# Linear attention and two MLPs on one core: 128-byte operand starts, weights in two pools, single group last

## The chip, the cores and the metric

The kernel runs on one core of a Trainium2 chip. The metric is the device time of one execution in microseconds (us). It is measured over several runs; one more execution is recorded by the hardware profiler, and all rows below come from that one.

The engines are TensorE (PE; its weight loads are listed as PEld), VectorE (DVE), ScalarE (ACT), GpSimd (POOL) and SyncE (SP), which issues the DMAs. Each engine works through its own instruction queue in order.

## The reference

```python
q_s = exp(q - max(q, -1));  q_s = q_s / (sum(q_s, -1) + 1e-9)      # q, k, v: 8 x 8 heads x 576 x 64, float32
k_s = exp(k - max(k, 2));   k_s = k_s / (sum(k_s, 2) + 1e-9)
kv  = einsum('bhsd,bhse->bhde', k_s, v)
x   = einsum('bhsd,bhde->bhse', q_s, kv)       # -> 4608 tokens x 512
h   = x @ w_in;  r = maximum(h, 0);  x = (r * r) @ w_out           # 512 -> 2048 -> 512, weights float64
g   = x @ w_gate;  val = x @ w_val                                 # 512 -> 1536
out = (g / (1 + exp(-g)) * val) @ w_out2                           # 1536 -> 512
```

## The kernel before

**First MLP.** The 4608 tokens go through in 9 blocks (`NB`) of 512 (`T`), the hidden width in 16 slices (`NF`). Every operand is kept as a high and a low part, and one product is three matmuls (`mm3`, L109). For each slice `f` of a block, `h_mm` makes 12 matmuls of 128x512 into the bank `ph`; `g_of` takes relu and square on ACT and splits the result into `g`, the low part on DVE (L104); one slice later `acc_mm` makes 12 matmuls into the four banks `acc`. The attention of the next block is worked in between by a plan.

**Weights.** The class `Weights` loads a raw float64 tile, takes its bits apart on ACT and DVE (`bits`, L136 to L146) and splits it on ACT and POOL (`split`, L187 and L189), all of this in block 0. The 32 split tiles live in the pool `wp` (32 slots of 4 KB per partition). The first 18 raw loads, and k, v and q of block 0, borrow slots of `wp` that no weight has taken yet; later raw loads go through `raws`, which has two buffers. Blocks 1 to 7 prepare the second MLP's weights (`operands`) and write them to DRAM.

**From one MLP to the other.** `x2_store` (L454) copies the four `acc` banks of a block to SBUF, two on ACT (L462) and two on DVE (L460), and SP stores each to DRAM `x2d` (L463). At the last block, 8, the attention's pools on the right side of SBUF are closed and `x1`, `wr` and `xs` take their place; from then on SP may fetch. The pools of the left side (`wr2`, `x2`, `st`, `uo`, `u`) lie where `wp` and its neighbours were, and open only when the first MLP is done.

**Second MLP.** It runs over groups of blocks with a scheme of seven products (order 1, 5, 6, 2, 7, 3, 4). The first group is the single block 0, and four pairs of blocks follow. `XOperands` loads a group's parts of `x2d` (L534) and makes its operands `xo` on ACT and DVE (L104, and `xt` and `x` in L542 to L552): in the last block of the first MLP for the first group, in the output stage of the group before for every other. `gated` makes 504 matmuls, 512 wide for a pair and 256 wide for the single; the two operands of a matmul are a slot `wu` and an `xo`. `out_stage` makes 504 (a pair) or 252 (the single), 256 wide, from `wu` and `uo`; each `uo` is split on ACT and DVE just before. `Stream` fetches `wu` tiles of 512 KB, 63 a group: 42 for `gated`, each used by 12 matmuls, and 21 for `out_stage`, each used by 24 (a pair) or 12 (the single). It runs up to 9 ahead (`LEAD`): of any nine consecutive tiles the first three (`EARLY`) lie in `wr`, the other six in `wr2`. Between the two MLPs `prime` writes one matmul into each of the eight banks (L571).

**What sets the order.** SP works in the order of the source. On the other engines a scheduler orders the instructions by readiness and program order when the kernel is built.

**Where tiles lie.** In the built program the pools of the left side start at multiples of 128 bytes in a partition. `pad` is the first allocation of the right side and shifts all that follow: with 8 floats it takes 64 bytes, so that `raws`, `cv` (bits), `stp`, `kp`, `qp`, `qtp`, and later `x1`, `wr` and `xs` start 64 bytes past a multiple of 128.

Of the kernel before, what the change touches and what calls it, by code (L numbers as in the profile page):

```python
# [17 lines left out]
P = 128  # L18
# [4 lines left out]
def tile_linear_attention_two_mlps(  # L23
# [34 lines left out]
    T = 512  # L58
# [15 lines left out]
    ph1 = ExitStack()  # L74
    wp = ph1.enter_context(tc.tile_pool(name="wp", bufs=2 * NF))
    rp = ph1.enter_context(tc.tile_pool(name="rp", bufs=2))
# [6 lines left out]
    pad = ctx.enter_context(tc.tile_pool(name="pad", bufs=1, side="right"))  # L83
    pad.tile([P, 8], F32, name="pad")
    raws = ph0.enter_context(tc.tile_pool(name="raws", bufs=2, side="right"))
# [65 lines left out]
    class Weights:  # L151
# [8 lines left out]
        def load(self):  # L160
            if self.n_load == len(self.order):
                return
            key = self.order[self.n_load]
            self.n_load += 1
            kind, f = key
            w = self.src[kind]
            if self.n_load <= self.borrow:
                t = w_slot(wp).rearrange("p t n -> p (t n)").bitcast(w.dtype)
            else:
                t = raws.tile([P, T], w.dtype, name="wraw", tag="wraw")  # L170
            raw_load(w, kind == "out", f, t)
            self.raw[key] = t
# [7 lines left out]
        def split(self, n):  # L180
            todo = []
            for key in self.order[self.n_split:min(self.n_split + n, self.n_bits)]:
                t = self.done[key] = w_slot(wp)
                self.n_split += 1
                todo.append((t, self.mid.pop(key)))
            for t, w in todo:
                nc.scalar.copy(t[:, 0], w)  # L187
            for t, w in todo:
                nc.gpsimd.tensor_tensor(t[:, 1], w, f32(t[:, 0]), op=ALU.subtract)  # L189
# [11 lines left out]
    def w_slot(pool):  # L201
        return pool.tile([P, 2, T], F32R, name="w", tag="w")
# [4 lines left out]
        + [x for f in range(NF) for x in (("out", f), ("in", f + 2)) if x[1] < NF],  # L207
        18,
    )
# [244 lines left out]
    def x2_store(i, d):  # L454
# [6 lines left out]
        else:  # L461
            nc.scalar.copy(e, acc.pop((i, d)))  # L462
        nc.sync.dma_start(x2d[i][:, d], e)  # L463


    groups = [(0,)] + [(i, i + 1) for i in range(1, NB, 2)]
    pools = {}
# [99 lines left out]
    def prime():  # L567
        t = stream.slots[0]
        banks = [bank() for _ in range(8)]
        for ps in banks:  # L570
            nc.tensor.matmul(  # L571
                ps, lhsT=t[:, 0, 0, 0:P], rhs=t.rearrange("p u t n -> p (u t n)")[:, 0:T],
                start=True, stop=True,
            )

# [109 lines left out]
    with tc.manual_schedule(engines={mybir.EngineType.SP}):  # L685
# [5 lines left out]
        def borrowed():  # L691
            return f32(w_slot(wp)).rearrange("p t n -> p (t n)")

# [20 lines left out]
        for hp, (n_kv, n_q, n_t, n_x) in enumerate(steps):  # L714
            plan.append((n_kv, lambda hp=hp: kv_unit(0, hp)))
            plan.append((n_q, lambda hp=hp: q_unit(0, hp)))
            plan.append((n_t, lambda hp=hp: q_transpose(0, hp, w_slot(wp))))
            plan.append((n_x, lambda hp=hp: x_pair(0, hp)))
# [9 lines left out]
        for n in range(NB * NF + LAG):  # L728
            i, f = divmod(n, NF)
            a = divmod(n - LAG, NF) if n >= LAG else None  # L730
            if i < NB:
                if f == 0:
# [6 lines left out]
                    if i == NB - 1:  # L739
# [3 lines left out]
                        for name, bufs in (("x1", 14), ("wr", EARLY), ("xs", 5)):  # L743
                            pools[name] = ctx.enter_context(
                                tc.tile_pool(name=name, bufs=bufs, side="right", reuse_waits="tile")
                            )
                        xo = XOperands(0)
                        xo.load(0)
                        for _ in range(EARLY):
                            stream.fetch()  # L750
                        steps = xo.all_steps()
                ph = h_mm(i, f)
# [4 lines left out]
                elif i < NB - 1 and n >= NF + 2:  # L757
                    next(work, None)
                if i == NB - 1 and f >= 2:
                    next(steps, None)  # L760
            if a and not (f == 0 and i < NB):
# [19 lines left out]

        prime()
        for _ in steps:
            pass
# [45 lines left out]
```

## Time and profile before

| | us |
|---|---|
| median of 3 runs (1749.21 to 1750.91) | 1750.1 |
| the profiled execution | 1751.04 |
| its span, first to last instruction | 1749.3 |
| PE busy in it | 1700.5 |
| DVE / ACT / POOL busy | 960.0 / 803.8 / 304.3 |

The profiled execution's time is 1.74 us longer than its span, and 0.9 us above the median. By the timeline, block 0 of the first MLP fills the first 160 us, the blocks 1 to 8 reach to 933 us, the single group to 1035 us, and each pair takes some 177 us after that. The mean granted clock of TensorE is 0.994 of full speed; a clock of 1.00 in a window is its higher level, 2.4 GHz, and 0.50 its lower one, 1.2 GHz.

### The profile page before, as it was taken

To read this page: it belongs to the slowest core of one execution; us is meant where nothing else is said; L and a number is where in the kernel's file an instruction comes from. 1 tells how busy PE (TensorE), PEld (TensorE's weight loads), DVE (VectorE), ACT (ScalarE), POOL (GpSimd) and SP (SyncE) were. 2 spreads that over 40 slices of the span, in tenths; PEclk is the share of its full clock that TensorE was granted. 3 is DMA by queue.
4 is the path that set the end of the run, shared out by engine and by line. 5 is a ranking of instruction groups with operands and counts; after the bars stand their busy time and mean duration, and the time that the engine had idled before them with its cause. 6 is when DMAs were issued, how large, how long until landed. Compare 5 with 4: busy or idle time off the path is not lost.

```text
span 1749.3 us, 25146 instructions
## 1 busy us (share of the span) xinstructions
PE 1700.5 (97%) x9420; PEld 1436.6 (82%) x9420; DVE 960.0 (55%) x1626; ACT 803.8 (46%) x1435; POOL 304.3 (17%) x279
## 2 busy tenths in 40 slices
PE   5889999999999999999999999999999999999999
PEld 4667888888888888888788988899889988998889
DVE  8997465555555555543412654475446544654455
ACT  5655444555555454554433453354335433543343
POOL 3552211112120211211001201210111011101110
PEclk9999999999999999999999989999999999999999
DMA  9344433434443343332206996668666866686663
GB/s 260 99 122 124 118 113 108 142 113 144 127 124 118 110 161 109 120 103 93 82 0 241 404 318 192 194 208 251 191 192 207 256 190 190 212 255 191 187 191 121
DMA packets 192969, 292.12 MB, mean 167 GB/s; under 512 B 87248, under 2 KB 124112, under 8 KB 192848
## 3 DMA queue, kind: packets, MB, share of 16 engines
q1 hardware_dynamic: 192848, 290.51, 53.3%
q8 instruction: 75, 1.23, 0.3%
q14 instruction: 46, 0.38, 0.1%
HBM read 238.55 MB, written 51.90 MB: 166 GB/s over the span
## 4 chain that ended last, share of the span: by engine, by line
PE 87%; DVE 4%; DMA 2%; issue 1%; ACT 1%; POOL 1%; SPq 0%; DVEq 0%; POOLq 0%; ACTq 0%
PE ps L109 45%; PE ph L109 20%; PE acc L109 20%; PE pa L339 1%; PE pa L374 1%; DVE wbits L142 1%; DVE wbits L146 1%; DMA wraw<-in_moe_w_out_dram 0%; POOL w L189 0%; DVE wbits L138 0%; DVE g L104 0%; DMA wu<-gvd 0%; DVE xo L104 0%; DMA x2d<-r 0%; DMA kt<-in_k_dram 0%
## 5 line engine op out<-in xcount | busy, mean ns | idle before, releaser
L109 PE MATMUL ps<-xo,wu 128*128 128x512 f32 (+1 forms) x2520 | 529.5, 372 | 0.1
L109 PEld LDWEIGHTS ps<-xo,wu 128*128 128x128 f32 x2520 | 439.2, 188 | 89.4 <-DMA wu<-gvd 0.3
L109 PE MATMUL acc<-g,w 128*128 128x512 f32 x1728 | 437.2, 398 | 5.5 <-DVE g L104 3.9
L109 PE MATMUL ph<-xT,w 128*128 128x512 f32 x1728 | 421.9, 393 | 10.1 <-POOL w L189 5.5
L109 PEld LDWEIGHTS ph<-xT,w 128*128 128x128 f32 x1728 | 321.1, 188 | 83.7 <-POOL w L189 7.6
L109 PEld LDWEIGHTS acc<-g,w 128*128 128x128 f32 x1728 | 318.4, 189 | 78.7 <-DVE g L104 8.3
L109 PE MATMUL ps<-wu,uo 128*128 128x256 f32 x2268 | 275.8, 284 | 4.4 <-DVE uo L104 3.1
L109 PEld LDWEIGHTS ps<-wu,uo 128*128 128x128 f32 x2268 | 274.3, 192 | 6.0 <-DVE uo L104 4.1
L104 DVE TENSOR_TENSOR g<-r,g 128x512 fp32r<-128x512 f32 x144 | 110.8, 770 | 187.9 <-ACT g L103 187.4
L442 ACT ACTIVATE r<-ph 128x512 f32<-128x512 f32 x144 | 85.8, 596 | 242.4 <-PE ph L109 235.0
L103 ACT CAST uo<-u 128x512 fp32r<-128x512 f32 (+1 forms) x210 | 119.2, 577 | 130.2 <-PE ps L109 88.2
L633 DVE TENSOR_TENSOR u<-u,ps 128x512 f32<-128x512 f32 (+1 forms) x60 | 38.0, 634 | 253.3 <-ACT u L632 253.0
L104 DVE TENSOR_TENSOR uo<-u,uo 128x512 fp32r<-128x512 f32 (+1 forms) x210 | 135.7, 657 | 63.8 <-ACT uo L103 63.4
L638 POOL TENSOR_TENSOR u<-u 128x512 f32<-128x512 f32 (+1 forms) x30 | 35.5, 1183 | 766.2 <-DVE u L634 627.9
L588 ACT COPY ps<-ps 128x512 f32<-128x512 f32 x126 | 71.9, 570 | 112.9 <-PE ps L109 110.9
L443 ACT ACTIVATE r<-r 128x512 f32<-128x512 f32 x144 | 91.1, 633 | 3.4
L103 ACT CAST g<-r 128x512 fp32r<-128x512 f32 x144 | 89.0, 618 | 3.3
L233 POOL TENSOR_TENSOR wsum<-wbits 128x256 f32<-128x256 f32 x36 | 35.0, 984 | 254.0 <-DVE wbits L146 198.9
L359 POOL TENSOR_TENSOR qs<-qs,qm 128x512 f32<-128x512 f32 x32 | 37.5, 1173 | 210.0 <-DVE qm L358 186.7
L189 POOL TENSOR_TENSOR w<-wbits,w 128x512 fp32r<-128x512 f32 x32 | 51.1, 1601 | 54.8 <-ACT w L187 49.1
L632 ACT ACTIVATE u<-ps 128x512 f32<-128x512 f32 (+1 forms) x60 | 33.3, 555 | 56.6 <-PE ps L109 56.5
L605 DVE TENSOR_TENSOR s<-ps,p 128x512 f32<-128x512 f32 x63 | 43.2, 690 | 26.8 <-PE ps L109 23.4
(99 smaller groups left out, 1383.2 us busy)
## 6 DMA issues: line engine op xcount, KB each, us to landing
wu<-gvd SPq DMA_DIRECT2D x210, 512.0 KB, 4.4
wu<-od SPq DMA_DIRECT2D x105, 512.0 KB, 4.0
gvd<-wst SPq DMA_DIRECT2D x84, 256.0 KB, 2.3
od<-wst SPq DMA_DIRECT2D x42, 256.0 KB, 2.3
wraw<-in_moe_w_out_dram SPq DMA_DIRECT2D x20, 512.0 KB, 4.3
x<-x2d SPq DMA_DIRECT2D x32, 256.0 KB, 6.0
kt<-in_k_dram SPq DMA_DIRECT2D x28, 288.0 KB, 3.3
vt<-in_v_dram SPq DMA_DIRECT2D x56, 144.0 KB, 3.7
```

The costliest lines, as they stand in the source:

```text
L103: nc.scalar.copy(hi, src)
L104: (eng or nc.vector).tensor_tensor(lo, src, f32(hi), op=ALU.subtract)
L109: nc.tensor.matmul(ps, lhsT=w[s], rhs=x[t], start=start and n == 0, stop=stop and n == 2, skip_group_check=more,)
L189: nc.gpsimd.tensor_tensor(t[:, 1], w, f32(t[:, 0]), op=ALU.subtract)
L233: nc.gpsimd.tensor_tensor(to, x, y, op=op)
L359: nc.gpsimd.tensor_tensor(t, t, m.unsqueeze(3).to_broadcast([P, TJ, 2, D]), op=ALU.subtract)
L442: nc.scalar.activation(r, ph, AF.Relu)
L443: nc.scalar.activation(r, r, AF.Square)
L588: nc.scalar.copy(x, y)
L605: nc.vector.tensor_tensor(x, y, z, op=ALU.add)
L633: nc.vector.tensor_tensor(u, u, gate, op=ALU.mult)
L638: nc.gpsimd.tensor_tensor(s1, a21, a22, op=ALU.add)
```

## The change

1. The pad takes 24 floats (128 bytes) instead of 8. All pools of the right side move by 64 bytes: `x1`, `wr`, `xs`, `raws`, `cv`, `stp`, `kp`, `qp` and `qtp` now start at multiples of 128. The attention's `kv` and `vt`, which stood there, are now 64 past.
2. The pool `wp` becomes two of 16 slots. `wpa` holds the weights of slices f < 8 and the borrowed raw loads (16 instead of 18), `wpb` those of f >= 8 and block 0's borrowed k, v, q and transposed q. `wr2`, `x2` and `st` lie on `wpa`, `uo` and `u` on `wpb` and above, so that the slots of `wr2` and `x2` come free halfway through block 8.
3. The groups are four pairs, and then block 8 alone. The first group is thus a pair: its operands are 512 wide, the loads 256 KB, and it needs the 14 tiles of `x2`.
4. The operands of the first group are emitted after the first MLP, not between the slices of block 8.
5. `x2_store` of block 8 issues its DMAs from ACT, not from SP.
6. `prime` writes two matmuls into the banks `pa` at the start of block 8, not eight into the second MLP's banks.

```diff
--- before.py
+++ after.py
@@ -72,7 +72,8 @@
     const = ctx.enter_context(tc.tile_pool(name="const", bufs=1))
     dram = ctx.enter_context(tc.tile_pool(name="dram", bufs=1, space=DRAM))
     ph1 = ExitStack()
-    wp = ph1.enter_context(tc.tile_pool(name="wp", bufs=2 * NF))
+    wpa = ph1.enter_context(tc.tile_pool(name="wpa", bufs=NF))
+    wpb = ph1.enter_context(tc.tile_pool(name="wpb", bufs=NF))
     rp = ph1.enter_context(tc.tile_pool(name="rp", bufs=2))
     gp = ph1.enter_context(tc.tile_pool(name="gp", bufs=2))
     xp = ph1.enter_context(tc.tile_pool(name="xp", bufs=NP))
@@ -81,7 +82,7 @@
     ps_a = ph1.enter_context(tc.tile_pool(name="ps_a", bufs=2, space=PSUM))
     ph0 = ExitStack()
     pad = ctx.enter_context(tc.tile_pool(name="pad", bufs=1, side="right"))
-    pad.tile([P, 8], F32, name="pad")
+    pad.tile([P, 24], F32, name="pad")
     raws = ph0.enter_context(tc.tile_pool(name="raws", bufs=2, side="right"))
     cv = ph0.enter_context(tc.tile_pool(name="cv", bufs=5, side="right"))
     stp = ph0.enter_context(tc.tile_pool(name="stp", bufs=1, side="right"))
@@ -165,7 +166,7 @@
             kind, f = key
             w = self.src[kind]
             if self.n_load <= self.borrow:
-                t = w_slot(wp).rearrange("p t n -> p (t n)").bitcast(w.dtype)
+                t = w_slot(wpa).rearrange("p t n -> p (t n)").bitcast(w.dtype)
             else:
                 t = raws.tile([P, T], w.dtype, name="wraw", tag="wraw")
             raw_load(w, kind == "out", f, t)
@@ -180,7 +181,7 @@
         def split(self, n):
             todo = []
             for key in self.order[self.n_split:min(self.n_split + n, self.n_bits)]:
-                t = self.done[key] = w_slot(wp)
+                t = self.done[key] = w_slot(wpa if key[1] < NF // 2 else wpb)
                 self.n_split += 1
                 todo.append((t, self.mid.pop(key)))
             for t, w in todo:
@@ -205,7 +206,7 @@
         {"in": w_in, "out": w_out},
         [("in", 0), ("in", 1)]
         + [x for f in range(NF) for x in (("out", f), ("in", f + 2)) if x[1] < NF],
-        18,
+        NF,
     )
 
 
@@ -460,10 +461,10 @@
             nc.vector.tensor_copy(e, acc.pop((i, d)))
         else:
             nc.scalar.copy(e, acc.pop((i, d)))
-        nc.sync.dma_start(x2d[i][:, d], e)
-
-
-    groups = [(0,)] + [(i, i + 1) for i in range(1, NB, 2)]
+        (nc.scalar if i == NB - 1 else nc.sync).dma_start(x2d[i][:, d], e)
+
+
+    groups = [(i, i + 1) for i in range(0, NB - 1, 2)] + [(NB - 1,)]
     pools = {}
     EARLY = 3
     LEAD = 9
@@ -565,13 +566,10 @@
 
 
     def prime():
-        t = stream.slots[0]
-        banks = [bank() for _ in range(8)]
-        for ps in banks:
-            nc.tensor.matmul(
-                ps, lhsT=t[:, 0, 0, 0:P], rhs=t.rearrange("p u t n -> p (u t n)")[:, 0:T],
-                start=True, stop=True,
-            )
+        w, x = w1.pair(("in", 0), 0), xT[NB - 1, 0]
+        for _ in range(2):
+            ps = ps_a.tile([P, T], F32, name="pa", tag="pa")
+            nc.tensor.matmul(ps, lhsT=w[0], rhs=x[:, 0], start=True, stop=True)
 
     def quarters(product, n):
 
@@ -689,7 +687,7 @@
 
 
         def borrowed():
-            return f32(w_slot(wp)).rearrange("p t n -> p (t n)")
+            return f32(w_slot(wpb)).rearrange("p t n -> p (t n)")
 
         for hp in range(NP):
             kt = borrowed()[:CK, 0:2 * NC * D].rearrange("p (h c d) -> p h c d", h=2, c=NC)
@@ -714,7 +712,7 @@
         for hp, (n_kv, n_q, n_t, n_x) in enumerate(steps):
             plan.append((n_kv, lambda hp=hp: kv_unit(0, hp)))
             plan.append((n_q, lambda hp=hp: q_unit(0, hp)))
-            plan.append((n_t, lambda hp=hp: q_transpose(0, hp, w_slot(wp))))
+            plan.append((n_t, lambda hp=hp: q_transpose(0, hp, w_slot(wpb))))
             plan.append((n_x, lambda hp=hp: x_pair(0, hp)))
         plan += [(5, lambda: w1.step(1)), (8, lambda: w1.step(1))]
         tick = run_at(plan)
@@ -744,11 +742,11 @@
                             pools[name] = ctx.enter_context(
                                 tc.tile_pool(name=name, bufs=bufs, side="right", reuse_waits="tile")
                             )
+                        prime()
                         xo = XOperands(0)
                         xo.load(0)
                         for _ in range(EARLY):
                             stream.fetch()
-                        steps = xo.all_steps()
                 ph = h_mm(i, f)
                 tick(2 * f)
                 g_of(i, f, ph)
@@ -756,8 +754,6 @@
                     w1.step(1)
                 elif i < NB - 1 and n >= NF + 2:
                     next(work, None)
-                if i == NB - 1 and f >= 2:
-                    next(steps, None)
             if a and not (f == 0 and i < NB):
                 for d in range(NP):
                     acc_mm(*a, d)
@@ -779,8 +775,7 @@
             tc.tile_pool(name="ps", bufs=8, space=PSUM, reuse_waits="tile")
         )
 
-        prime()
-        for _ in steps:
+        for _ in xo.all_steps():
             pass
         for g in range(len(groups)):
             ops, steps, after = [], iter(()), None
```

The order of the instructions moves with it at three places. The first is PE (a) and ACT (b) between the MLPs and after; `acc` and `ph` are banks of the first MLP, `ps` those of the second, and `xN` counts like instructions in a row. PE before, from the last slice of block 8 to the second pair:

```order
L109 MATMUL ph<-xT,w 128x512 x12
L109 MATMUL acc<-g,w 128x512 x24
L571 MATMUL ps<-wu 128x512 x8
L109 MATMUL ps<-xo,wu 128x256 x504
L109 MATMUL ps<-wu,uo 128x256 x252
L109 MATMUL ps<-xo,wu 128x512 x504
L109 MATMUL ps<-wu,uo 128x256 x504
L109 MATMUL ps<-xo,wu 128x512 x504
```

PE now, over the rest of the program:

```order
L110 MATMUL ph<-xT,w 128x512 x12
L110 MATMUL acc<-g,w 128x512 x24
L110 MATMUL ps<-xo,wu 128x512 x504
L110 MATMUL ps<-wu,uo 128x256 x504
L110 MATMUL ps<-xo,wu 128x512 x504
L110 MATMUL ps<-wu,uo 128x256 x504
L110 MATMUL ps<-xo,wu 128x512 x504
L110 MATMUL ps<-wu,uo 128x256 x504
L110 MATMUL ps<-xo,wu 128x512 x504
L110 MATMUL ps<-wu,uo 128x256 x504
L110 MATMUL ps<-xo,wu 128x256 x504
L110 MATMUL ps<-wu,uo 128x256 x252
```

The eight matmuls of `prime` are gone from between the MLPs, and the single group's 256-wide gated matmuls stand last. ACT at the same place before (the copies of `acc` for `x2d`, and then the seeding of banks):

```order
L442 ACTIVATE r<-ph 128x512
L443 ACTIVATE r<-r 128x512
L103 CAST g<-r 128x512
L462 COPY r<-acc 128x512 x2
L588 COPY ps<-ps 128x512
L597 COPY p_8220<-ps 128x512
L588 COPY ps<-ps 128x512
```

ACT now:

```order
L444 ACTIVATE r<-r 128x512
L104 CAST g<-r 128x512
L463 COPY r<-acc 128x512
L464 DMA x2d_125<-r 128x512 x2
L463 COPY r<-acc 128x512
L464 DMA x2d_125<-r 128x512 x2
L586 COPY ps<-ps 128x512 x2
L595 COPY p_8230<-ps 128x512
L595 COPY p_8231<-ps 128x512
```

The stores of block 8 (`x2d_125`) stand in ACT's queue between the copies and the first seeding. SP at the start of block 8, before (`x2d_114` is block 0, `x2d_121` and `x2d_122` are blocks 7 and 8):

```order
L534 DMA x<-x2d_114 128x256 x4
L487 DMA wu<-gvd_123 128x1024 x3
L463 DMA x2d_121<-r 128x512 x4
L534 DMA x<-x2d_114 128x256 x4
L463 DMA x2d_122<-r 128x512 x4
L487 DMA wu<-gvd_123 128x1024 x4
L487 DMA wu<-gvd_124 128x1024 x7
```

SP now (`x2d_117`, `x2d_118` and `x2d_124` are blocks 0, 1 and 7):

```order
L535 DMA x<-x2d_117 128x512
L535 DMA x<-x2d_118 128x512 x2
L535 DMA x<-x2d_117 128x512
L488 DMA wu<-gvd_126 128x1024 x3
L464 DMA x2d_124<-r 128x512 x4
L535 DMA x<-x2d_117 128x512
L535 DMA x<-x2d_118 128x512 x2
L535 DMA x<-x2d_117 128x512
L488 DMA wu<-gvd_126 128x1024 x4
L488 DMA wu<-gvd_127 128x1024 x7
```

Eight loads of 128 KB have become eight of 256 KB, and no store stands between the loads and the fetches of `wu`. DVE in the second half of block 8, before, where the operands of the single group (128x256) go on past the copies for block 7's store:

```order
L104 TENSOR_TENSOR g<-r,g 128x512
L545 TENSOR_TENSOR x<-x 128x256
L104 TENSOR_TENSOR xo<-x,xo 128x256
L104 TENSOR_TENSOR g<-r,g 128x512
L104 TENSOR_TENSOR xo<-xt,xo 128x256
L547 TENSOR_TENSOR x<-x 128x256
L104 TENSOR_TENSOR xo<-x,xo 128x256
L552 TENSOR_TENSOR x<-x 128x256
L104 TENSOR_TENSOR xo<-x,xo 128x256 x4
L104 TENSOR_TENSOR g<-r,g 128x512 x13
L460 COPY r<-acc 128x512 x2
```

DVE now, in the slices f 8 to 15 of block 8:

```order
L105 TENSOR_TENSOR g<-r,g 128x512
L105 TENSOR_TENSOR xo<-x,xo 128x512
L543 TENSOR_TENSOR xt<-x 128x512
L546 TENSOR_TENSOR x<-x 128x512
L105 TENSOR_TENSOR xo<-xt,xo 128x512
L548 TENSOR_TENSOR x<-x 128x512
L105 TENSOR_TENSOR xo<-x,xo 128x512
L553 TENSOR_TENSOR x<-x 128x512
L105 TENSOR_TENSOR xo<-x,xo 128x512
L105 TENSOR_TENSOR g<-r,g 128x512
L105 TENSOR_TENSOR xo<-x,xo 128x512 x3
L105 TENSOR_TENSOR g<-r,g 128x512 x5
```

The first `g` here is that of slice 9. Nine operand steps stand just before it, behind the `g` of slice 8; eight stand between it and the next, and three behind that one.

## Rows read from the trace of the kernel before

**Rows 1.** page, part 1 busy time, and part 4 the chain by line.

```profile
PE 1700.5 (97%) x9420; PEld 1436.6 (82%) x9420; DVE 960.0 (55%) x1626; ACT 803.8 (46%) x1435; POOL 304.3 (17%) x279
...
PE ps L109 45%; PE ph L109 20%; PE acc L109 20%; PE pa L339 1%; PE pa L374 1%; DVE wbits L142 1%; DVE wbits L146 1%; DMA wraw<-in_moe_w_out_dram 0%; POOL w L189 0%; DVE wbits L138 0%; DVE g L104 0%; DMA wu<-gvd 0%; DVE xo L104 0%; DMA x2d<-r 0%; DMA kt<-in_k_dram 0%
```

**Rows 2.** windows, PE alone: us, PE busy (matmuls touched), granted clock, DMA share, GB/s.

```profile
870.00:930.00 60.00, 60.00 (x266) 1.00 0.00 1
1050.00:1150.00 100.00, 100.00 (x433) 1.00 0.66 200
1160.00:1200.00 40.00, 40.00 (x338) 1.00 0.70 223
```

**Rows 3.** windows, PE, cut at weight slots: gated pair (two), output stage (two).

```profile
1070.24:1086.78 16.54, 16.54 (x72) 1.00 0.63 186
1087.01:1095.04 8.03, 8.03 (x36) 1.00 0.66 186
1153.76:1162.29 8.53, 8.53 (x72) 1.00 0.57 184
1162.40:1170.77 8.37, 8.37 (x73) 1.00 0.57 180
```

**Rows 4.** timeline, first MLP to second: start us, us, what, [idle before <-releaser].

```profile
...
933.29 0.85 PE L571 MATMUL ps<-wu 128*128 128x512 f32 x3
...
935.75 1.42 PE L571 MATMUL ps<-wu 128*128 128x512 f32 x5 [1.61 <-DVE r L460]
...
937.01 5.22 PE L109 MATMUL ps<-xo,wu 128*128 128x256 f32 x39
...
941.61 0.54 PEld L109 LDWEIGHTS ps<-xo,wu 128*128 128x128 f32 x4 [0.33 <-DMA wu<-gvd]
```

**Rows 5.** timeline of PE, output stage of the single group.

```profile
996.75 5.50 PE L109 MATMUL ps<-wu,uo 128*128 128x256 f32 x44
...
1005.08 24.84 PE L109 MATMUL ps<-wu,uo 128*128 128x256 f32 x190 [0.20 <-DVE uo L104]
...
1033.12 2.50 PE L109 MATMUL ps<-wu,uo 128*128 128x256 f32 x10 [2.37 <-DVE uo L104]
1035.42 4.88 PE L109 MATMUL ps<-xo,wu 128*128 128x512 f32 x13
```

**Rows 6.** chain of waits inside that output stage: start us, us, what.

```profile
...
999.19 1.14 DVE xt L542
...
1029.12 1.21 DVE xo L104 x2
...
```

**Rows 7.** windows, PE alone: transition, single group, first pair, a later pair.

```profile
933.00:942.00 9.00, 7.26 (x49) 1.00 0.78 241
950.00:990.00 40.00, 40.00 (x342) 1.00 1.03 408
1010.00:1020.00 10.00, 10.00 (x86) 1.00 0.94 301
1035.10:1038.50 3.40, 3.40 (x11) 0.50 0.95 304
1213.00:1223.00 10.00, 10.00 (x51) 1.00 0.80 249
```

**Rows 8.** start of the last block: timeline of PE, and the page's DMA issues.

```profile
856.12 2.11 PE L109 MATMUL ph<-xT,w 128*128 128x512 f32 x8 [1.27 <-ACT r L442]
...
x<-x2d SPq DMA_DIRECT2D x32, 256.0 KB, 6.0
...
x<-x2d SPq DMA_DIRECT2D x8, 128.0 KB, 3.2
```

**Rows 9.** timeline of DVE, late in the last block.

```profile
924.48 0.69 DVE L104 TENSOR_TENSOR g<-r,g 128x512 fp32r<-128x512 f32 x1 [4.75 <-ACT g L103]
```

**Rows 10.** timeline of ACT at the end.

```profile
1744.71 1.30 ACT L678 COPY o<-ps 128x512 f32<-128x512 f32 x2 [7.30 <-PE ps L109]
```

**Rows 11.** windows, all engines, block 0: PE, PEld, DVE, ACT, POOL busy, clock, DMA.

```profile
0.00:160.00 160.00, 124.91 (x653) 93.00 (x653) 140.26 (x224) 89.53 (x161) 72.08 (x61) 0.97 0.57 154
```

## The prediction

> **What bounds the kernel now.** I read the page first: PE is busy 1700.5 of 1749.3 us, and 85% of the chain that ended last are three lines of matmuls [rows 1]. So a term counts only if it shortens matmuls, or fills a gap between them; DVE, ACT and the DMA queue matter where PE waits for them. The other views serve to find both. Windows of PE alone give the spacing of matmuls in each stage: the first MLP makes 266 of 512 columns in 60 us, a pair's gated stage 433 in 100 us, its output stage 338 of 256 columns in 40 us [rows 2]. A window also counts the matmuls that it cuts, one too many, so these are 60/265 = 226.4 ns, 100/432 = 231.5 ns and 40/337 = 118.7 ns. Timelines then show where PE stands still: between the MLPs [rows 4], in the single group's output stage [rows 5], and at the start of block 8 [rows 8]. I sum against the profiled execution's 1751.04 us, and take 0.9 off at the end, since the median lies so much lower.
>
> **Alignment (change 1).** In the first MLP all operands of a matmul start at multiples of 128 bytes. In a gated stage `xo` of `x1` lies 64 bytes past, and the slot alternates: the 72 matmuls on six `wr2` slots, which are aligned, took 16.54 us, the 36 on three `wr` slots, 64 past like `x1`, took 8.03 us [rows 3]. These windows run from the first start to the last, so there are 71 and 35 spacings: 232.9 and 229.4 ns. In the output stage `uo` is aligned: with `wr2`, all aligned, 8.53/71 = 120.1 ns; with `wr`, mixed, 8.37/71 = 117.9 ns (72 starts, and one cut) [rows 3]. So for 512 columns a mixed pair is the slowest, for 256 it is the fastest. After the change everything in the second MLP is aligned.
> The pairs' 2016 gated matmuls go from 231.6 ns (2/3 of 232.9 and 1/3 of 229.4 make 231.7; the long window said 231.5) to a value that this trace shows in the first MLP alone: 226.4 would give 2016 x 5.2 = 10.5 us, the 229.4 of two operands displaced alike 4.4 us, and no effect 0. I take 227.5, nearer to the one row in which all is aligned, since that row has the same shape and three-product pattern: 2016 x 4.1 = **-8.3 us**.
> The 256-wide ones lose. A third of the 2268 output matmuls are on `wr`: 756 x 2.2 = 1.7 us. The single's 504 gated ones took from 937.01 to 996.75, 59.74 us [rows 4, 5], less 0.3 of waiting 117.9 ns each; at 120.1 they cost 1.1 us more. Sum **+2.8 us**; bounds 0 to 2.8. Net **-5.5 us**, between -10.5 and +2.8.
> Other engines and DMAs on these pools I cost at nothing: only PE is on the path, and its spacing in the gated stage is the same at a DMA share of 0.63 and 0.66 [rows 3].
> The Trainium skill, page "SBUF — State Buffer", section "Specifications (TRN2)", says that a partition is read in lines of 16 bytes, and that bandwidth is lost where a line isn't hit at least twice. By that a start at 64 is as good as one at 128, and this term would be 0. The trace speaks against it: rows of one shape and engine differ by 1.5 and 1.9% with the slot alone [rows 3].
>
> **Between the MLPs (changes 2, 5, 6).** Before, the last `acc` matmul ends where `prime` begins, at 933.29; three go, PE waits 1.61 us for the DVE copy of the last bank, which waited for a store, five more go, and the first real one starts at 937.01; at 941.61 a weight load waits 0.33 us for a `wu`, whose fetch stood behind the stores in SP's queue [rows 4]. That is 3.7 + 0.3 = 4.0 us. After, the first product needs the banks of the first two copies, which are out by 933, and `wu` tiles that have long been there. What is next late: the seeding copies on ACT, now behind the block's last copy and store in ACT's own queue (its order stands ahead). Product 1 is 12 matmuls, 2.75 us, and lasts to 936.05; the next in line waits for the seeds. ACT copies the last bank at about 934.3 as before (it waits for the same buffer), and then the issue and two copies of 0.57 us follow, done by 936.75: a wait of 0.7 us (0 if the scheduler's next product goes first, 1.5 if the issue on ACT takes longer). The two matmuls of `prime` at the start of block 8 cost 0.46 us if nothing hides them. Net -4.0 + 0.7 + 0.5 = **-2.9 us** (-4.0 to -1.5).
>
> **The single group last (change 3).** Its output stage makes 252 matmuls of 256 columns. They ran from 996.75 to 1035.42, 38.67 us [rows 5], where 252 x 118.7 ns = 29.9 us would do: 8.7 us lost. The next group's first matmuls ran at a granted clock of 0.50 from 1035.10 to 1038.50 [rows 7]: 3.4 us for 1.7 us of work. Sum 10.4 us. The chain inside that stage is DVE at `xt`, `x` and `xo` of the following pair [rows 6], 512 wide, which stand ahead of the single's own `uo`: the next group's operands are a pair's, and the cover is half a pair's long. From pair to pair the same work is covered: 1213 to 1223 shows PE full at clock 1.00 [rows 7]. After, the single is followed by nothing, and the pair before it has to make only half-width operands. I take all of it, **-10.3 us** (-10.4 to -8).
>
> **Start of block 8 (changes 3, 4).** SP loads 4 x 256 KB before the `wu` fetches and block 7's stores, instead of 4 x 128 KB; such a load took 6.0 us instead of 3.2 [rows 8]. The stores land later by up to the difference of the transfer, half of 2.8 us, since the loads overlap: +1.4. The copies of block 7's last banks wait for them, then `g`, then PE, which waited 1.27 us there [rows 8]. The next loads and the steps of c = 1 no longer stand ahead of `g` there, -0.6. Together **+0.8 us** (0 to +2).
>
> **Middle of block 8 (change 4).** Nine operand steps stand on DVE between the `g` of slices 8 and 9, eight more before slice 10. A `g` takes 0.69 us, and DVE then waits 4.75 us for the next [rows 9]; nine steps of 0.69 take 6.2 us, 1.5 more than the gap. Since a slice's `acc` matmuls come one slice later, PE has 12 matmuls, 2.7 us, before it needs that `g`. So covered, but for the loads of c = 1, which six `wu` fetches press on: **+0.3 us** (0 to +2.5).
>
> **The end.** PE stops, two banks are copied on ACT one after the other (1.30 us [rows 10]) and stored. With the single there is one: **-0.3 us**. **Block 0** is paced by DVE, 140.26 of 160 us, with PE at 124.91 [rows 11]; weights now wait for other slots, two raw loads more go through `raws`, and q loads of the next block stand behind them on SP. The first split may come earlier. I find nothing that makes a sign: **0 us**, between -3 and +3.
>
> **Sum.** -5.5 - 2.9 - 10.3 + 0.8 + 0.3 - 0.3 = -17.9: 1751.04 - 17.9 = 1733.1, on the median's footing **1732 us**.
>
> **Rivals.**
> (a) The alignment brings nothing, neither gain nor loss: 5.5 more, 1738. Against it, the slots' rows; for it, that the two operands displaced alike [rows 3] are not the slowest.
> (b) The gated stage reaches the first MLP's spacing fully: 2.2 less, and with the seeds in time 1729.
> (c) The single's stalls belong to its half-length products, and move to the end with it; change 3 doesn't do what it seems to: 10.3 more, 1742. Against it, the names in the chain [rows 6], none of them its own but `uo`.
> (d) Slower: the single group at the end starves. Its 63 tiles are 33.0 MB for 504 x 120 + 252 x 119 ns = 90 us; nine are there ahead, so 54, 28.3 MB, must come at 314 GB/s. In 950 to 990 it got 408 GB/s with PE full, at a DMA share of 1.03, which is all there is; in 1010 to 1020 301 GB/s [rows 7]. At 301 it takes 94 us, 4 us more. It decides from 262 GB/s: 28.3 MB then take 108 us, all 17.9 us are gone, and any less is slower than before, 1752 at 257. Nothing in the rows is so low while PE waits for `wu`.
> (e) The clock falls between the MLPs, where no `prime` keeps PE at work: some 3.4 us at half speed as in 1035.10 to 1038.50 [rows 7], 1.7 more, 1734. For it, the 2.37 us without work ahead of that stretch [rows 5]. Against it, the wait of 1.61 us between the MLPs, after which the clock stayed at 1.00 [rows 4, 7]; the wait that I expect is shorter. [...]
>
> **How the numbers follow.** Forecast 0.62, (a) 0.12, (b) 0.09, (c) 0.08, (d) 0.03, (e) 0.06. The low end takes the alignment at its bound and a gain in block 0: 1732 - 5 - 2 = 1725; the high end takes (a) with block 0 against it: 1738 + 3 = 1741. Outside lie (c), (d) and some tails, 0.2 in all. A difference under 0.2%, 3.5 us, could not be told from no change. All but (d) lie below 1746.6; with tails: faster 0.93, same 0.04, slower 0.03.
>
> **What would show it.** Right: gated windows of pairs at about 440 matmuls in 100 us, PE without a gap between product 1 and the last `acc`, the output stages full from the first pair to the end, no clock below 1.00 behind 160 us. Wrong: gated windows still at 433; gaps in the single's output stage with no `xo` in their chain; weight loads that wait for `wu` in the last 90 us; a first MLP's block 0 that ends later than at 160 us.

## The result, and the profile after

The changed kernel takes 1732.4 us in the median of 4 runs (1730.23 to 1733.91), the kernel before 1749.65 beside it: a ratio of 0.9901, 95% interval 0.9884 to 0.9918. The forecast was 1732. The profiled execution of the changed kernel has a span of 1732.1 us at a mean granted clock of 0.998. It lies 17.2 us below the span before, and the accounts below are made between these two spans. The profiled execution was the slowest of the four runs, at 1733.9 us; on that footing the forecast was 1733.1.

From the page of the changed kernel, the busy time of each engine and the chain by line; they answer to [rows 1]:

```profile
PE 1686.0 (97%) x9414; PEld 1434.3 (83%) x9414; DVE 960.6 (55%) x1626; ACT 803.7 (46%) x1435; POOL 297.8 (17%) x279
...
PE ps L110 45%; PE ph L110 21%; PE acc L110 19%; PE pa L340 1%; DVE wbits L147 1%; DVE wbits L143 1%; PE pa L375 1%; POOL w L190 1%; DMA x2d<-r 1%; DVE wbits L139 1%; DVE m L320 1%; DVE g L105 0%; DMA wraw<-in_moe_w_out_dram 0%; ACT wbits L137 0%; DMA x<-x2d 0%
```

PE is still what the kernel consists of: 14.5 us less of PE's time, and 2.7 us less without it.

Windows of PE alone (us, PE busy and matmuls touched, granted clock, DMA share, GB/s): the stretch between the MLPs, a pair's gated stage, a pair's output stage, and the single's two stages, which now end the program. They answer to [rows 2] and [rows 7]:

```profile
933.00:945.00 12.00, 11.24 (x49) 1.00 0.39 132
1120.00:1220.00 100.00, 100.00 (x443) 1.00 0.69 205
1060.00:1100.00 40.00, 40.00 (x336) 1.00 0.73 226
1640.00:1690.00 50.00, 50.00 (x419) 1.00 0.98 366
1698.00:1727.00 29.00, 29.00 (x244) 1.00 0.81 299
```

443 matmuls in 100 us where 433 were, so 226.2 ns each, or 226.7 by a stage's own length (114.27/504; before 116.85/504 = 231.8); in the output stage 60.48/504 = 120.0 ns, before 60.17/504 = 119.4. The single group runs at 366 GB/s with PE full, and its output stage, 244 in 29 us, has no gap.

The program by stages. Each boundary is the first matmul of a stage in a timeline of PE, in block 1 the first `g` on DVE:

| stage | before, us | after, us | difference |
|---|---|---|---|
| start to first `g` of block 1 | 166.43 | 169.48 | +3.05 |
| from there to the second MLP's first matmul | 770.58 | 767.94 | -2.64 |
| four gated stages of pairs | 469.13 | 458.13 | -11.00 |
| four output stages of pairs | 240.85 | 241.89 | +1.04 |
| gated stage of the single | 59.74 | 60.48 | +0.74 |
| output stage of the single | 38.67 | 30.40 | -8.27 |
| end of PE to end of span | 3.90 | 3.78 | -0.12 |
| sum | 1749.3 | 1732.1 | -17.2 |

Timeline between the MLPs after (start, length, what, and in brackets the idle time before with its releaser), the place of [rows 4]:

```profile
...
937.42 2.88 PE L110 MATMUL ps<-xo,wu 128*128 128x512 f32 x12
938.67 0.59 ACT L463 COPY r<-acc 128x512 f32<-128x512 f32 x1 [2.54 <-DMA x2d<-r]
939.29 1.11 ACTq L464 DMA_DIRECT2D x2d<-r  x2
939.35 0.69 DVE L461 COPY r<-acc 128x512 f32<-128x512 f32 x1 [2.42 <-DMA x2d<-r]
...
940.44 1.06 ACT L586 COPY ps<-ps 128x512 f32<-128x512 f32 x2 [1.18 <-PE ps L110]
...
941.07 2.11 PE L110 MATMUL ps<-xo,wu 128*128 128x512 f32 x8 [0.76 <-ACT ps L586]
```

There is no `prime` and no gap ahead of the first product. ACT's queue is as forecast: copy, two stores, where the second waits for DVE's copy at 939.35, and only then the seeding copies; PE waits 0.76 us for these at 941.07.

Block 8 after, its start, the place of [rows 8]:

```profile
...
857.76 1.79 PE L110 MATMUL acc<-g,w 128*128 128x512 f32 x6 [1.31 <-ACT r L463]
860.54 2.09 PE L110 MATMUL ph<-xT,w 128*128 128x512 f32 x8 [0.99 <-ACT r L443]
...
```

and its middle, PE and then DVE; the gap ahead of `g` in [rows 9] is filled:

```profile
...
910.24 2.76 PE L110 MATMUL acc<-g,w 128*128 128x512 f32 x11 [0.21 <-DVE g L105]
...
```

```profile
...
903.48 0.69 DVE L543 TENSOR_TENSOR xt<-x 128x512 f32<-128x512 f32 x1 [0.38 <-DMA x<-x2d]
904.81 0.69 DVE L546 TENSOR_TENSOR x<-x 128x512 f32<-128x512 f32 x1 [0.63 <-DMA x<-x2d]
...
909.50 0.68 DVE L105 TENSOR_TENSOR g<-r,g 128x512 fp32r<-128x512 f32 x1
...
```

DVE waits 0.38 and 0.63 us for `x` loads of c = 1, `g` of slice 10 comes at 909.50, and PE waits 0.21 us for it.

Block 0, DVE's first `g` of block 1 and SP's last raw load of the first MLP's weights; the first stood at 166.43 before, the other at 143.31:

```profile
169.48 0.69 DVE L105 TENSOR_TENSOR g<-r,g 128x512 fp32r<-128x512 f32 x1 [3.49 <-ACT g L104]
```

```profile
...
146.62 0.35 SPq L118 DMA_DIRECT2D wraw<-in_moe_w_out_dram  x1
```

### The profile page after: what moved, and what is told of

Same layout as the page of the kernel before. It is cut to its first block, busy times and chain, and to the rows that moved or that the text cites. A ratio compares the mean times of both kernels' runs of the same rounds, so it can differ in the third digit from the quotient of the medians.

```text
span 1732.1 us, 25141 instructions
## 1 busy us (share of the span) xinstructions
PE 1686.0 (97%) x9414; PEld 1434.3 (83%) x9414; DVE 960.6 (55%) x1626; ACT 803.7 (46%) x1435; POOL 297.8 (17%) x279
## 4 chain that ended last, share of the span: by engine, by line
PE 88%; DVE 5%; DMA 2%; ACT 2%; issue 2%; POOL 1%; SPq 0%; ACTq 0%; POOLq 0%; DVEq 0%
PE ps L110 45%; PE ph L110 21%; PE acc L110 19%; PE pa L340 1%; DVE wbits L147 1%; DVE wbits L143 1%; PE pa L375 1%; POOL w L190 1%; DMA x2d<-r 1%; DVE wbits L139 1%; DVE m L320 1%; DVE g L105 0%; DMA wraw<-in_moe_w_out_dram 0%; ACT wbits L137 0%; DMA x<-x2d 0%
## 5 line engine op out<-in xcount | busy, mean ns | idle before, releaser
L110 PE MATMUL ps<-xo,wu 128*128 128x512 f32 (+1 forms) x2520 | 518.7, 368 | 0.8 <-ACT ps L586 0.8
L110 PE MATMUL ph<-xT,w 128*128 128x512 f32 x1728 | 427.4, 396 | 13.6 <-POOL w L190 5.6
L105 DVE TENSOR_TENSOR g<-r,g 128x512 fp32r<-128x512 f32 x144 | 106.7, 741 | 183.1 <-ACT g L104 182.8
L190 POOL TENSOR_TENSOR w<-wbits,w 128x512 fp32r<-128x512 f32 x32 | 45.9, 1438 | 68.8 <-ACT w L188 66.3
L595 ACT COPY p<-ps 128x512 f32<-128x512 f32 x63 | 37.0, 588 | 42.6 <-PE ps L110 41.7
```

The costliest lines, as they stand in the source:

```text
L105: (eng or nc.vector).tensor_tensor(lo, src, f32(hi), op=ALU.subtract)
L110: nc.tensor.matmul(ps, lhsT=w[s], rhs=x[t], start=start and n == 0, stop=stop and n == 2, skip_group_check=more,)
L595: nc.scalar.copy(x, y)
```

## The experiments

Each kernel ran beside the kernel before on the same chip. Times are medians, and in brackets stands the median of the kernel before on that chip, which is 1748.3 to 1749.65 us. Differences to the changed kernel are taken from its 1732.4; counted by the distance to the kernel before beside each, they come out up to 1.4 us larger.

**Alignment alone, on the kernel before.**

```diff
-    pad.tile([P, 8], F32, name="pad")
+    pad.tile([P, 24], F32, name="pad")
```

> The kernel before with one edit: the pad takes 24 floats. Theory (alignment sets the spacing of matmuls): the 2016 gated 512-wide matmuls of the pairs go from 231.8 to 226.7 ns each, -10.3 us; the 256-wide ones lose 2 us; 1749.6 becomes about 1741.5, and block 1's first g stays at 166 us. Rival 1 (the spacing came from the new order or the pools): gated spacing stays at 231.8, time 1749.6. Rival 2 (the 3 us that block 0 lost came with the moved raw and bits tiles): spacing as in the theory, but block 1's first g at 169 us, time about 1744.5.

1740.7 us (1748.3), ratio 0.9948, interval 0.9932 to 0.9965. Its windows of a gated and of an output stage:

```profile
1220.00:1320.00 100.00, 100.00 (x443) 1.00 0.65 205
1160.00:1200.00 40.00, 40.00 (x336) 1.00 0.70 223
```

443 and 336, the counts of the changed kernel, in an order and in pools that are those of before. Block 1's first `g` stands at 166.20. So the spacing comes from the start addresses of the right side's tiles alone. That is worth 7.6 us here, and both rivals fall.

**Alignment taken back, on the changed kernel.**

```diff
-    pad.tile([P, 24], F32, name="pad")
+    pad.tile([P, 8], F32, name="pad")
```

> The changed kernel with the pad back at 8 floats. Theory (alignment): gated spacing of pairs back at 231.8 ns, output stages at 119.4, time 1732.4 + 8.3 = 1740.7; block 1's first g stays near 169 us, since the pools and the 16 borrowed loads cost that. Rival (block 0's 3 us belong to the alignment): first g of block 1 back at 166 us, time about 1737.6.

1740.7 us (1748.3), 8.3 more than the changed kernel's 1732.4. Windows of a gated and an output stage of a pair, and of the single's gated stage:

```profile
1120.00:1220.00 100.00, 100.00 (x433) 1.00 0.64 200
1060.00:1100.00 40.00, 40.00 (x338) 1.00 0.69 222
...
1650.00:1700.00 50.00, 50.00 (x435) 1.00 1.00 382
```

433 and 338 again, as in [rows 2]. The single's gated stage, 256 wide, makes 435 in 50 us, where aligned operands made 419. Cut at the slots, first six of `wr2` and then three of `wr`:

```profile
1651.00:1659.05 8.05, 8.05 (x74) 1.00 0.94 365
1659.16:1663.36 4.20, 4.20 (x38) 1.00 1.02 408
```

These windows run from the first start to the last of 72 and of 36 matmuls, and count two more that are still running when they open. That is 8.05/71 = 113.4 ns on `wr2`, where `xo` alone lies 64 past, and 4.20/35 = 120.0 ns on `wr`, where both do. For 256 columns two operands displaced alike are as slow as two aligned ones, and a mixed pair is quicker. Block 1's first `g` stays at 169.70, so its 3 us do not come with the addresses.

**The single group first again, on the changed kernel.**

```diff
-    groups = [(i, i + 1) for i in range(0, NB - 1, 2)] + [(NB - 1,)]
+    groups = [(0,)] + [(i, i + 1) for i in range(1, NB, 2)]
```

> The changed kernel with block 0 alone as the first group again. Theory (the single's output stage is too short for DVE to make a pair's operands in it): its 252 output matmuls take 38 us again instead of 30, the next pair starts at half clock, and the time is 1732.4 + 10.4, less up to 1 for lighter loads at the start of block 8: about 1742. Rival (the gain of the order lay elsewhere): within 2 us of 1732.4.

1736.6 us (1748.3): slower by 4.2 than with the single last (5.5 by the distance to the kernel before), not by 10. Timeline of PE over its output stage, and a window over the start of the pair behind it, the places of [rows 5] and [rows 7]:

```profile
...
997.25 4.72 PE L110 MATMUL ps<-wu,uo 128*128 128x256 f32 x38
...
1031.01 1.46 PE L110 MATMUL ps<-wu,uo 128*128 128x256 f32 x10 [2.37 <-DVE uo L105]
1032.30 9.94 PE L110 MATMUL ps<-xo,wu 128*128 128x512 f32 x43
```

```profile
1030.00:1040.00 10.00, 8.99 (x44) 1.00 0.96 339
```

The stage takes 35.05 us, from 997.25 to 1032.30, where it took 38.67 before and takes 30.40 when last. The wait of 2.37 us near its end is that of [rows 5]; the waits at its start are smaller than there, and the pair behind it starts at clock 1.00. The mechanism is there, at under half of the price.

**The same, with the pair's operand steps behind the stage.** On top of the last edit:

```diff
-            out_stage(g, ops, lambda: (next(steps, None), next(steps, None)))
+            out_stage(g, ops, (lambda: None) if g == 0 else (lambda: (next(steps, None), next(steps, None))))
```

> Single group first as in the run above, but the operand steps of the pair behind it are emitted behind the single's output stage, so that on DVE the splits of the stage itself go ahead where both are ready, and the second half of the loads starts late. Theory (the stage stalls because these steps stand ahead of its own splits): its 252 output matmuls take 30 to 32 us, not 35, and PE then waits 8 to 16 us for the pair's operands: about 1741 to 1749. Rival (a half-length stage stalls by itself): the stage still takes 35 us or more.

1743.7 us (1748.7). Timeline of PE:

```profile
...
997.45 30.40 PE L110 MATMUL ps<-wu,uo 128*128 128x256 f32 x252
1027.69 1.55 PE L110 MATMUL ps<-xo,wu 128*128 128x512 f32 x6
1036.92 18.29 PE L110 MATMUL ps<-xo,wu 128*128 128x512 f32 x65 [7.68 <-ACT xo L104]
```

All 252 output matmuls in one run of 30.4 us, and then 7.68 us of waiting for the first operands of c = 1. The half-length stage doesn't stall by itself. It stalls because another group's operand steps stand ahead of its own splits on DVE, and where they don't, the group behind waits. The steps of c = 0 still run in the stage here, behind the splits; those of c = 1 come after it, so that order and amount of the steps were not taken apart.

**The same, with the low halves on POOL.** The single first, and the second group's 14 low halves on POOL:

```diff
-        split(hi, lo, src)
+        split(hi, lo, src, eng)
...
+            self.eng = nc.gpsimd if g == 1 else None
...
```

> As the run with the single group first, but the low halves of the second group's operands are made on POOL, not on DVE: 14 of DVE's 26 steps in the single's output stage go. Theory (DVE's work for the next pair causes the stalls): the output stage of the single shrinks from 38 us to 30 to 33, time 1733 to 1737. Rival (a half-length group stalls by itself, its splits come too close to their use): the stage stays at 38 us, time about 1742.

1739.7 us (1748.3), 3.1 more than with these halves on DVE; the stage takes 40.2 us. By the expectation that spoke against DVE as the cause, but the run took another turn. Timelines of DVE and of POOL in it:

```profile
...
1022.36 0.42 DVE L105 TENSOR_TENSOR uo<-u,uo 128x256 fp32r<-128x256 f32 x1 [0.29 <-ACT uo L104]
1022.70 0.68 DVE L544 TENSOR_TENSOR xt<-x 128x512 f32<-128x512 f32 x1
1023.30 1.52 DVE L105 TENSOR_TENSOR uo<-u,uo 128x256 fp32r<-128x256 f32 x1
1024.74 1.78 DVE L547 TENSOR_TENSOR x<-x 128x512 f32<-128x512 f32 x1
1026.44 1.49 DVE L105 TENSOR_TENSOR uo<-u,uo 128x256 fp32r<-128x256 f32 x1
1027.86 0.68 DVE L549 TENSOR_TENSOR x<-x 128x512 f32<-128x512 f32 x1
...
```

```profile
...
1022.92 1.62 POOL L105 TENSOR_TENSOR xo<-x,xo 128x512 fp32r<-128x512 f32 x1 [14.36 <-DMA wu<-od]
1024.50 1.47 POOL L105 TENSOR_TENSOR xo<-xt,xo 128x512 fp32r<-128x512 f32 x1
1025.93 1.73 POOL L105 TENSOR_TENSOR xo<-x,xo 128x512 fp32r<-128x512 f32 x1
...
```

A `uo` of 0.42 us takes 1.52 and 1.49 us, and the step of L547 (0.68 us elsewhere) 1.78 us, all between 1023 and 1028, when POOL makes `xo`. At 1022.70 and 1027.86 the same kinds take 0.68. DVE got fewer steps and slower ones. As a test of the cause this run decides nothing; the run ahead of it does.

**Block 8's stores back on SP.**

```diff
-        (nc.scalar if i == NB - 1 else nc.sync).dma_start(x2d[i][:, d], e)
+        nc.sync.dma_start(x2d[i][:, d], e)
```

> The changed kernel with block 8's stores on SP again, where they stand ahead of the first pair's second operand loads (c = 1) and of the fetches into the second weight pool. Theory (SP would wait there for the last copies): the c = 1 loads are issued only at about 936 us, land at 942, the operands follow, and PE stands some 9 to 12 us between the MLPs: about 1743. Rival (the loads are early enough, or hidden behind the first products): within 2 us of 1732.4.

1740.9 us (1749.4), 8.5 more than the changed kernel. Timelines of SP and of PE:

```profile
936.09 4.08 SPq L464 DMA_DIRECT2D x2d<-r  x4
940.22 1.89 SPq L535 DMA_DIRECT2D x<-x2d  x4
...
```

```profile
...
944.67 4.01 PE L110 MATMUL ps<-xo,wu 128*128 128x512 f32 x9 [5.80 <-ACT xo L104]
949.66 2.56 PE L110 MATMUL ps<-xo,wu 128*128 128x512 f32 x10 [0.99 <-DMA wu<-gvd]
```

SP issues the four stores from 936.09 and only then the loads of c = 1; PE makes the six matmuls of c = 0 and waits 5.80 us for an operand, and later for `wu`. The queue of the stores is an edit of one line; to take it back costs half of what the whole change brings.

**One pool of weights.** The changed kernel with `wp` of 32 slots and 18 borrowed loads:

```diff
-    wpa = ph1.enter_context(tc.tile_pool(name="wpa", bufs=NF))
-    wpb = ph1.enter_context(tc.tile_pool(name="wpb", bufs=NF))
+    wp = ph1.enter_context(tc.tile_pool(name="wp", bufs=2 * NF))
...
-        NF,
+        18,
...
```

> The changed kernel with one pool of 32 weight slots and 18 borrowed loads, as before; the low halves of the first pair's operands then lie on weights that are read to the end. Theory (the split of the pool is what lets the pair go first): the operand steps of the first pair start at about 932 us, PE stands 8 to 15 us between the MLPs, some of it is repeated at half clock; block 0 gets its 3 us back: about 1739. Rival (the first products hide these steps): 1730.

1735.9 us (1749.4), with runs from 1734.0 to 1740.4; the profiled one is the slowest of them, with a span of 1738.6. Timeline of PE in that one, and a window of PE behind the wait:

```profile
...
942.47 1.22 PE L109 MATMUL ps<-xo,wu 128*128 128x512 f32 x2 [4.04 <-ACT xo L103]
944.02 16.27 PE L109 MATMUL ps<-xo,wu 128*128 128x512 f32 x59 [0.33 <-DVE xo L104]
```

```profile
942.47:950.00 7.53, 7.18 (x17) 0.58 0.85 259
```

The second MLP starts with six matmuls, and 4.04 us of waiting follow; its first gated stage takes 7 us longer than in the changed kernel, with 4.4 us of waits where that has 0.8, and a mean clock of 0.58 behind them. Block 0 is quicker by 3.65, its first `g` of block 1 at 165.83. The split of the pool is what lets the pair go first without a gap. Block 0 pays a part of it with 16 borrowed loads; with 18 and the split it does not, as the run with 18 on the changed kernel below shows. The gap came out below the 8 to 15 us that I expected: six matmuls run ahead of it, and operand steps run on DVE beside them.

**Two primes, on the kernel before.** The changed kernel's `prime` in place of the eight matmuls:

```diff
-        banks = [bank() for _ in range(8)]
-        for ps in banks:
...
+        for _ in range(2):
+            ps = ps_a.tile([P, T], F32, name="pa", tag="pa")
...
+                        prime()
...
-        prime()
         for _ in steps:
```

> The kernel before with the changed kernel's prime: two matmuls at the start of block 8 in place of eight between the MLPs. Theory (the fetches behind block 8's stores set the time between the MLPs, not prime): PE starts the second MLP at about 933.5, has three tiles, and then waits for the fourth until 941 as before; time 1749.6 within 1. Rival (prime itself cost the 4 us): about 1746.

1749.7 us (1749.4), ratio 1.000, interval 0.9991 to 1.001. Timeline between the MLPs, and a window of PE behind the wait:

```profile
...
929.26 4.14 SPq L463 DMA_DIRECT2D x2d<-r  x4
...
930.51 4.47 PE L109 MATMUL ps<-xo,wu 128*128 128x256 f32 x36
...
933.49 8.80 SPq L487 DMA_DIRECT2D wu<-gvd  x10
...
939.01 3.35 PE L109 MATMUL ps<-xo,wu 128*128 128x256 f32 x14 [4.04 <-DMA wu<-gvd]
...
```

```profile
939.01:943.99 4.98, 4.98 (x24) 0.51 1.02 418
```

PE begins the second MLP at 930.51 with no gap, uses up three tiles in 36 matmuls, and then waits 4.04 us for the fourth, which SP could issue only at 933.49, behind the stores. The eight matmuls of `prime` and their wait cost the kernel before nothing: they stood in this wait. They may even have helped there. Without them the clock falls behind the wait, and from the last `acc` to the single's output stage this trace takes 65.08 us (930.51 to 995.59), against 63.46 before (933.29 to 996.75). The equal time is thus a balance: the stretch ahead of it, from the first `g` of block 1 on, is 2.3 us shorter here (764.57 against 766.86), for a reason that no run here shows.

**18 borrowed loads, on the changed kernel.** The first 11 raw loads in `wpa`, 12 to 18 in `wpb`:

```diff
-                t = w_slot(wpa).rearrange("p t n -> p (t n)").bitcast(w.dtype)
+                t = w_slot(wpa if self.n_load <= 11 else wpb).rearrange("p t n -> p (t n)").bitcast(w.dtype)
...
-        NF,
+        18,
```

> The changed kernel with 18 borrowed raw loads again, the first 11 in the lower pool, 12 to 18 in the upper one on the slots that k, v and q of block 0 leave. Theory (block 0 lost 3 us because two loads more go through the two raw buffers): first g of block 1 back from 169 to about 166 us, time about 1729.4. Rival (block 0 differs for another reason, or by chance): first g stays at 169, time 1732.4.

1731.4 us (1749.4), ratio 0.9898, interval 0.9882 to 0.9915. DVE's first `g` of block 1 and SP's last raw load in its trace:

```profile
166.88 0.69 DVE L105 TENSOR_TENSOR g<-r,g 128x512 fp32r<-128x512 f32 x1 [3.49 <-ACT g L104]
```

```profile
...
142.25 0.35 SPq L118 DMA_DIRECT2D wraw<-in_moe_w_out_dram  x1
```

The load is issued 4.4 us sooner than in the changed kernel and the `g` comes 2.6 us sooner. Since this is less than the times of runs differ, it ran again, with the changed kernel beside it:

> The changed kernel once more, unaltered, beside the two that follow: its own median on this chip, 1730 to 1734 by its runs so far, and first g of block 1 near 169 us in another profile.

> The kernel with 18 borrowed loads once more, unaltered, in more runs. Theory (two loads more through the raw buffers cost block 0 3 us): 2 to 3 us below the changed kernel of the same call. Rival (chance): the same within 1 us.

1732.3 us for the changed kernel (1748.7; 1731.05 to 1734.81), 1731.3 for the 18 loads (1729.38 to 1735.82). By the traces the first `g` of block 1 is at 165.6 to 167.1 us in the seven traces of kernels with 18 borrowed loads, that of the kernel before among them, and at 167.7 to 170.6 us in the seven with 16. By the times the gain is 1 us in both calls, which the runs don't resolve. So that block 0 loses some 3 us in the traces with 16 borrowed loads is shown; that it is the two raw buffers, and not also the slots that loads 12 to 16 now wait for, was not taken apart, as the edit changes both.

**And two stores on POOL.** On top of that, the second and fourth store of block 8 from POOL:

```diff
-        (nc.scalar if i == NB - 1 else nc.sync).dma_start(x2d[i][:, d], e)
+        ((nc.gpsimd if d % 2 else nc.scalar) if i == NB - 1 else nc.sync).dma_start(x2d[i][:, d], e)
```

> The kernel with 18 borrowed loads, and of block 8's four stores the second and fourth issued from POOL instead of ACT. In the changed kernel's trace ACT's queue holds the store of the fourth bank, which waits for DVE's last copy, ahead of the seeding copies, and PE waits 0.76 us for these. Theory (that store holds the seeds up): the wait goes, 0.8 us less than with 18 borrowed loads alone. Rival (ACT's own last copy, which waits for a buffer, sets it): no change.

1731.1 us (1748.7; 1729.14 to 1733.24), ratio 0.9899, interval 0.9884 to 0.9913. Timeline between the MLPs:

```profile
...
935.05 7.28 PE L110 MATMUL ps<-xo,wu 128*128 128x512 f32 x31
...
937.12 0.57 ACT L586 COPY ps<-ps 128x512 f32<-128x512 f32 x1 [0.40 <-ACT r L463]
...
```

The seeding copy now starts at 937.12, right behind ACT's own second store, and the 31 matmuls from 935.05 run without a wait. So it was the fourth bank's store, waiting in ACT's queue for DVE's copy, that held the seeds. In the time it can't be told from the kernel without it. This version is the lowest of all medians, 1.3 us below the changed kernel of the same call, and not shown to be faster than it.

## Why the prediction was right

The time came out within 0.4 us of the forecast (0.8 by the profiled executions), but two of its terms were off by 2 to 3 us, in opposite directions. Point by point, by the steps of the forecast:

- **What bounds it** held: PE's time and PE's gaps carry the whole difference.
- **Alignment**, forecast -5.5: the trace gives -8.0. Of the pairs' -11.0 us, 1.7 are the half clock at [rows 7] that went, and 0.8 the new wait for seeds goes the other way: -10.1 by spacing, 231.8 to 226.7 ns. The output stages give +1.0, the single +0.74, and 0.3 more for a wait there that went. The term was mis-sized at one choice: 227.5 ns, between the first MLP's 226.4 and the other rows, where the first MLP's row was the answer, and rival (b) the right case for this term. Its reading of [rows 3] was also coarser than the layout. A pair's `xo` has its high half in `x1` and its low half in `x2` (`x_split`), and `x2` starts at a multiple of 128 in both kernels. One matmul of three reads the low half, so the 232.9 and 229.4 ns called mixed and displaced alike are averages of two kinds. The loss of the 256-wide ones, forecast +2.8, is +2.1: in the output stage 119.4 became 120.0, since `wr` holds only 6 of its 21 tiles, not a third, and their matmuls lost 2.1 ns each. The rule of the Trainium skill, page "SBUF — State Buffer", section "Specifications (TRN2)", from which rival (a) was made, doesn't explain these 5 ns: with the starts moved by 64 bytes, a whole number of its 16-byte lines, and nothing else, the spacing moved. Why the start of an operand matters to TensorE, no run here shows.
- **Between the MLPs**, forecast -2.9: the 3.7 us gap went, 0.3 of waiting for `wu` went, 0.76 for the seeds came, and the two matmuls of `prime` at the start of block 8 take 0.46 (846.14 to 846.60), as reckoned: -2.8. The named cause of the new wait was the right one, as the run with stores on POOL shows. What the forecast did not see is that the eight matmuls of `prime` weighed nothing themselves. It counted them in a gap that the late fetches would have made anyway; the gain is the fetches', so the stores' queue and the early slots'.
- **The single group last**, forecast -10.3: the trace gives 8.3 and 1.7, -10.0. The cause is as named. But the order alone, with the rest of the change in place, is worth 4.2 us. The other 5 or so vanish with the single still first, because DVE's order in that stage is another and the clock holds; with the pad alone on the kernel before, the stage still takes 38.6 us. Which of pools, early fetches and emission moved it was not tested.
- **Start and middle of block 8**, forecast +1.1: 770.58 to 767.94 is -2.64, of which the gap is -3.72 and `prime` +0.46. That leaves +0.6 for all of blocks 1 to 8, and it is not resolved: the changed kernel's second trace has 769.66 for the 767.94.
- **Block 0**, forecast 0 between -3 and +3: +3.05 in the profiled run, just past the edge; its sign of being wrong, a block 0 that ends later, came true. "I find nothing that makes a sign" was the step that failed: two raw loads more through two buffers and weights that wait for other slots stood in the text and were put at nothing, and the kernels with 18 borrowed loads give the 3 us back in their traces.
- **The end**, forecast -0.3: -0.12.
- **Rivals.** (a) fell to the two runs with the pad. (c) fell to the changed kernel itself and to the run with the steps behind the stage. (d): the single at the end moves 366 GB/s with PE full, above the 314 that it needs. (e): the clock holds at 1.00 between the MLPs, where PE's longest wait is 0.76 us. Its mechanism is real: behind the waits of 4.04 us in the runs with two primes and with one pool the clock did fall.

The two misses, -2.5 in the alignment and +3 in block 0, nearly cancel. The agreement to 0.4 us is in part that.

## What to carry to other kernels

Where matmuls of one shape show two spacings that alternate with a buffer, look at the start addresses of both operands: 64 bytes of padding moved 5 ns a matmul here, and it is a test of one line. A small stage next to a large one is where to look for stalls, since work that is made ahead during a stage is sized by the next one, not by it. Before a gap is credited to the instructions that stand in it, remove them and see what waits then: here a DMA queue stood behind them.

## What the runs showed of the hardware

- Matmuls of 512 columns between fp32r tiles took 226.7 ns with all operands at multiples of 128 bytes. With the high half of `xo` 64 past and its low half aligned, they averaged 232.9 ns on aligned `wu` slots and 229.4 on slots 64 past [rows 3].
- For 256 columns, 120.0 ns aligned in the changed kernel's single gated stage, 120.0 with both operands 64 past and 113.4 with one, in the run with the pad taken back. The size is not fixed: that run's whole stage averages 58.31/504 = 115.7 ns, the kernel before with the same starts 117.9.
- Elementwise work on DVE took up to 3.6 times as long (0.42 to 1.52 us) while POOL worked on SBUF tiles too.
- A wait of 2.37 us on PE at the end of the single's output stage was followed by 0.50 of the clock in the kernel before [rows 5, 7], and by 1.00 when the same wait stood in the changed kernel with the single first. The length of the last wait alone does not tell whether the clock falls.
